# Rows of x, logits and routing matmuls of two groups of batches in the score banks of PSUM

## The chip, the core and the metric

The kernel runs on one core of one Trainium2 chip (trn2). The engines are PE (TensorE, the matmul engine), DVE (VectorE), ACT (ScalarE), POOL (GpSimd) and SP (SyncE, which here only issues DMAs). The metric is the device time of one execution in microseconds, the lower the better; three runs of the kernel before are shown, and one more execution was profiled.

## What is computed

Sparse attention of 8 batches, 8 heads, 576 positions and 64 dimensions a head is followed by a mixture of experts in which every token goes to one expert. Heads 0 to 3 see a local window of 32 positions, heads 4 to 7 every 32nd position. Cut to what matters:

```
scores = scale * q @ k.T                       # per batch and head
scores = where(mask, scores, -1e9)             # local (heads 0-3) or strided (heads 4-7)
attn   = softmax(scores) @ v
x      = attn.transpose(0, 2, 1, 3).reshape(4608, 512)
logits = x @ w_gate                            # 8 experts
expert, gate = argmax(logits), softmax(logits)[argmax]
for e in range(8):
    xe = x[expert == e]
    out[expert == e] = gate * (relu(xe @ w1[e]) @ w2[e])   # 512 -> 1024 -> 512
```

All is fp32. The expert products are made from two parts of each operand, a rounded one (hi) and the rest (lo), with three matmuls for each product: hi x hi, lo x hi, hi x lo.

## The kernel before

**Attention as tasks.** A task is one score bank: 512 columns that hold several blocks of queries and keys of one batch. Each batch has five (`BANK_PAIRS`), so there are 40 tasks in all; tasks 3 and 4 of a batch are scored together (`PAIR`). In one turn of the loop PE scores a task (mask matmul L439, then L450, L458 or L464), transposes the probabilities of the task three turns ago (L501, `LAG_T`) and multiplies those of the task four turns ago with V (L526 for local heads, L515 for strided ones, `LAG_AV`). Between a task's scores and its transposes stands the softmax: DVE takes the maximum (nm, L377) and subtracts it (prob, L380, the last reader of the score bank), ACT takes the exponential (L381), DVE sums (sm, L383; ri, L385 and L386), POOL multiplies (L387). ACT copies the products with V to xT (L166), which holds x of two batches, transposed.

**What follows a group.** Two batches make a group, so there are four. When a batch of a group is through, its *logits* (PE L576 with the gate's weights wg, DVE's copy ls at L162, PE's transposes L583, DVE's sum L584), its *rows of x* (`xrows`: PE transposes xT at L568, ACT copies the bank to xr at L166, a DMA issued by ACT at L571 writes the rows to xd in DRAM) and, after the second batch, the *route* (rank of each token in its expert: PE L618 and L620, DVE rk L623; lists of token numbers: PE L666, DVE idacc L669) are worked in small steps between the tasks of the following batches.

**Early experts.** From the third group on, PE's time between attention steps is filled with windows of experts 0, 2, 4 and 6 over the tokens of the first two groups. A window gathers rows of xd (xg, on POOL), transposes them (PE L296, in a v bank), splits them (ACT xh L240, DVE xl L241), and for each of four chunks of weights loads raw (1 MB, issued by SP at L221), splits it (ACT whi L231, DVE wlo L232, two halves each), makes the hidden product (PE L320 to L322 in a t bank), splits that (ACT hh L325, DVE hl L326) and makes the second product (PE L309 to L311 in y banks). At the end y is scaled (DVE L276 or ACT L274) and scattered by POOL.

**Tables and the rest.** When all groups are routed, `slot_tables` works out which tokens the remaining windows and slots take (DVE almost alone: the function from L727 on, with comparisons L803 and L808 at its end and PE's L812 in v banks for each group), between steps of the last early window and the first window of expert 0. Then come windows and slots of all experts to the end.

**PSUM.** All eight banks are given out by four tags with two banks each (`BANKS`, L58): s for scores, t for transposes and hidden products, v for products with V, and y for second products. A tag's two banks take turns, so an allocation waits until the content of the allocation two before it has been read. `XTAGS` (L59) gives, for each of the four groups, the tag that `xrows`, `logits` and `route` allocate.

**Order.** In the attention loop PE's order is the order of the program text (`tc.manual_schedule`). The orders of DVE, ACT, POOL and SP, and PE's after the loop, are made by the scheduler of the build, which estimates when each instruction could start. On the chip each engine runs its row in that order and waits where something isn't ready.

Of the kernel before, what the change touches and what calls it, by code (L numbers as in the profile page):

```python
# [55 lines left out]
X_ENG = "aa"  # L56
LS_ENG = "v"
BANKS = {"s": 2, "t": 2, "v": 2, "y": 2}  # L58
XTAGS = "yyvv"  # L59
YTAGS = "yyss"  # L60
PRE = (0, 2)
BANK_PAIRS = (
# [85 lines left out]
def moe_attn(ctx, tc, qk, vv, wg, wcat, blob0, blob, out):  # L148
# [8 lines left out]
    def bank(tag):  # L157
        return ps.tile([128, 512], F32, name=tag, bufs=BANKS[tag])
# [186 lines left out]
    with ExitStack() as actx:  # L345
# [217 lines left out]
        def xrows(g, c, xT):  # L563
            xr = xrp.tile([128, XW], F32, name="xr")
            nc.gpsimd.tensor_copy(out=xr[:, DM:XW], in_=gates[g][:, c:c + 1].broadcast_to([128, XW - DM]))
            xb = bank(XTAGS[g])
            for pr in range(4):
# [5 lines left out]
        def logits(g, c3, xT, L):  # L573
            lb = bank(XTAGS[g])
            for pr in range(4):
                nc.tensor.matmul(lb[32 * pr:32 * pr + 32, 0:384], wg_sb[:, pr, :], xT[:, pr, c3 * 384:(c3 + 1) * 384],  # L576
                                 start=True, stop=True, tile_position=(0, 32 * pr))
            ls = rt.tile([128, 384], F32, name="ls", bufs=2)
            evac(LS_ENG, ls, lb[:, 0:384])
            yield  # L580
            lt = bank(XTAGS[g])
            for i in range(3):
                nc.tensor.transpose(lt[:, i * 128:(i + 1) * 128], ls[:, i * 128:(i + 1) * 128], ident)  # L583
            nc.vector.tensor_reduce(out=L[:, 3 * c3:3 * c3 + 3, :],  # L584
                                    in_=lt[:, 0:384].rearrange("p (t q e) -> p t e q", t=3, q=4)[:, :, 0:E, :],
                                    axis=AX.X, op=ALU.add)
            cs = slice(3 * c3, 3 * c3 + 3)
            mx = rt.tile([128, 3], F32, name="mx", bufs=2)
            nc.vector.tensor_reduce(out=mx, in_=L[:, cs, :], axis=AX.X, op=ALU.max)
            dl = dls[g][:, cs, :]  # L590
            nc.vector.tensor_tensor(out=dl, in0=L[:, cs, :], in1=mx.unsqueeze(2).broadcast_to([128, 3, E]), op=ALU.subtract)
            ex = rt.tile([128, 3, E], F32, name="ex", bufs=2)
            nc.scalar.activation(out=ex, in_=dl, func=AF.Exp)
            yield
            gt = gates[g][:, cs]
            nc.vector.tensor_reduce(out=gt, in_=ex, axis=AX.X, op=ALU.add)
            nc.vector.tensor_scalar(out=gt, in0=gt, scalar1=1e-9, scalar2=None, op0=ALU.add)
            nc.vector.reciprocal(out=gt, in_=gt)
# [4 lines left out]
        def route(g):  # L603
# [9 lines left out]
            if g < NG - 1:  # L613
                yield
                yield
            rb = bank(XTAGS[g])
            rv = rb[:, 0:(GT + 1) * E].rearrange("p (c e) -> p c e", e=E)
# [43 lines left out]
            if g < NG - 1:  # L661
                yield
                yield
            ib = bank(XTAGS[g])
            for c in range(GT):
# [634 lines left out]
```

## Time and profile before

| | us |
|---|---|
| three runs: median (lowest to highest) | 630.91 (630.07 to 633.26) |
| the profiled execution | 629.62 |
| its span from first to last instruction | 627.7 |
| PE busy in the span | 589.2 (94%) |
| DVE busy | 374.2 (60%) |
| ACT busy | 296.3 (47%) |
| POOL busy | 159.3 (25%) |

The profile gives for each engine the time in which it ran instructions; waiting for a semaphore, issuing a DMA and branches aren't counted. Times in the trace are counted from the start of the span. An execution lasts 1.9 us longer than its span. PE is the busiest engine over the whole span, but the shares differ by stage: the last two groups of batches are worked from about 107 to 226 us, the tables from 226 to 268, the remaining windows from there to the end.

### The profile page before, as it was taken

What the parts mean: (1) busy time and instruction counts of PE and PEld (TensorE: products, weight loads), DVE (VectorE), ACT (ScalarE), POOL (GpSimd) and SP (SyncE); (2) the same over time, 40 slices, a digit from 0 to 9 for tenths busy, and PEclk for the clock granted to TensorE, in tenths of its full rate; (3) what the DMA queues carried; (4) which work ended last, traced back from release to release, by engine and by line L of the source; (5) the groups of instructions that cost most, each with busy time, mean ns of one, the idle gap of its engine ahead of it and who ended that gap; (6) DMA issues with size and microseconds to landing.
All of it is one profiled execution on the core that took longest, in us unless ns stands there. A gap on an engine that the chain in (4) does not pass through costs nothing. (4 is left out here: it accounts for less than half of the span.)

```text
span 627.7 us, 14487 instructions
## 1 busy us (share of the span) xinstructions
PE 589.2 (94%) x5973; PEld 491.2 (78%) x5986; DVE 374.2 (60%) x744; ACT 296.3 (47%) x523; POOL 159.3 (25%) x195
## 2 busy tenths in 40 slices
PE   4898897899889999899999999999999999999996
PEld 3676765678778888797888898788998878887885
DVE  6779989877573699987325855233634334551332
ACT  1676767754665544555325744233533324442241
POOL 3333432530230303146302432022412004020021
PEclk9999999999899999989999999999999999999999
DMA  8888999986458657469934774375655538253201
GB/s 316 269 307 294 300 359 317 374 299 237 158 176 314 209 191 244 153 229 331 393 144 149 250 263 172 117 252 187 212 191 184 173 105 296 107 175 144 69 32 58
DMA packets 33540, 137.25 MB, mean 219 GB/s; under 512 B 4666, under 2 KB 5056, under 8 KB 24768
## 3 DMA queue, kind: packets, MB, share of 16 engines
q1 hardware_dynamic: 19840, 93.33, 43.3%
q10 hardware_dynamic: 7344, 22.71, 9.9%
q0 software_dynamic: 6288, 20.26, 8.8%
q8 instruction: 48, 0.79, 0.5%
q14 instruction: 20, 0.16, 0.1%
HBM read 117.11 MB, written 19.63 MB: 218 GB/s over the span
## 5 line engine op out<-in xcount | busy, mean ns | idle before, releaser
L232 DVE TENSOR_TENSOR wlo<-raw,whi 128x1024 fp32r<-128x1024 f32 x112 | 135.0, 1225 | 69.7 <-ACT whi L231 67.5
L231 ACT CAST whi<-raw 128x1024 fp32r<-128x1024 f32 x112 | 114.2, 1050 | 58.2 <-PE s L311 39.8
L320 PE MATMUL t<-xh,whi 128*128 128x256 f32 (+2 forms) x384 | 131.8, 344 | 2.9 <-DVE hl L326 1.6
L322 PE MATMUL t<-xh,wlo 128*128 128x256 f32 (+2 forms) x384 | 128.1, 334 | 0.6 <-DVE wlo L232 0.6
L321 PE MATMUL t<-xl,whi 128*128 128x256 f32 (+2 forms) x384 | 128.1, 334 | 0.0
L326 DVE SCALAR_TENSOR_TENSOR hl<-t,hh 128x256 fp32r<-128x256 f32 (+2 forms) x96 | 52.0, 542 | 116.3 <-ACT hh L325 116.2
L325 ACT ACTIVATE hh<-t 128x256 fp32r<-128x256 f32 (+2 forms) x96 | 46.4, 483 | 138.8 <-PE t L322 137.7
L320 PEld LDWEIGHTS t<-xh,whi 128*128 128x128 f32 x384 | 72.6, 189 | 13.1 <-issue 3.2
L322 PEld LDWEIGHTS t<-xh,wlo 128*128 128x128 f32 x384 | 72.8, 190 | 6.2 <-DVE wlo L232 0.9
L321 PEld LDWEIGHTS t<-xl,whi 128*128 128x128 f32 x384 | 72.8, 190 | 6.2 <-DVE xl L241 0.3
L310 PE MATMUL y<-wlo,hh 128*128 128x512 f32 x192 | 76.0, 396 | 0.9 <-DVE wlo L232 0.9
L309 PE MATMUL y<-whi,hh 128*128 128x512 f32 x192 | 76.8, 401 | 0.0
L311 PE MATMUL y<-whi,hl 128*128 128x512 f32 x192 | 75.6, 396 | 0.0
L387 POOL TENSOR_TENSOR prob<-prob,ri 128x512 f32<-128x512 f32 x40 | 43.2, 1088 | 101.2 <-DVE ri L386 62.0
L277 POOL DMA_INDIRECT out_dram<-y,oids x27 | 29.7, 1099 | 106.0 <-DVE y L276 100.5
L249 POOL DMA_INDIRECT xg<-xd,ids x27 | 33.4, 1238 | 75.2 <-PE v L296 38.5
L311 PEld LDWEIGHTS y<-whi,hl 128*128 128x128 f32 x192 | 36.2, 189 | 8.3 <-DVE hl L326 0.8
L310 PEld LDWEIGHTS y<-wlo,hh 128*128 128x128 f32 x192 | 36.5, 190 | 6.5 <-DVE wlo L232 1.4
L309 PEld LDWEIGHTS y<-whi,hh 128*128 128x128 f32 x192 | 36.6, 191 | 5.8
L166 ACT COPY xT<-v 128x270 f32<-128x270 f32 (+1 forms) x80 | 29.2, 484 | 18.0 <-PE v L515 9.4
L381 ACT ACTIVATE prob<-prob 128x512 f32<-128x512 f32 x40 | 25.0, 632 | 20.4 <-DVE prob L380 20.1
L310 PE MATMUL s<-wlo,hh 128*128 128x512 f32 x88 | 34.6, 393 | 0.0
(226 smaller groups left out, 904.2 us busy)
## 6 DMA issues: line engine op xcount, KB each, us to landing
raw<-in_wcat_dram SPq DMA_DIRECT2D x56, 1024.0 KB, 5.3
sraw<-in_wcat_dram ACTq DMA_DIRECT2D x12, 1024.0 KB, 4.9
xd<-xr ACTq DMA_DIRECT2D x36, 264.0 KB, 4.0
qkl<-in_qk_dram SPq DMA_DIRECT2D x32, 264.0 KB, 4.8
vl<-in_vv_dram SPq DMA_DIRECT2D x16, 512.0 KB, 6.2
vt<-in_vv_dram SPq DMA_DIRECT2D x16, 256.0 KB, 5.8
qk<-in_qk_dram SPq DMA_DIRECT2D x8, 484.0 KB, 6.4
qk<-in_qk_dram SPq DMA_DIRECT2D x8, 432.0 KB, 5.6
```

The costliest lines, as they stand in the source:

```text
L231: nc.scalar.copy(out=hi[:, sl], in_=raw[:, sl])
L232: i = nc.vector.tensor_tensor(out=lo[:, sl], in0=raw[:, sl], in1=hi[:, sl].bitcast(F32), op=ALU.subtract)
L249: lastp[0] = nc.gpsimd.indirect_dma_start(out=xg, out_offset=None, in_=xd[0:rows, :], in_offset=bass.IndirectOffsetOnAxis(ap=idc, axis=0))
L309: nc.tensor.matmul(yb[t], hh[:, ts], whi[:, w], start=(j == 0), stop=False)
L310: nc.tensor.matmul(yb[t], hh[:, ts], wlo[:, w], start=False, stop=False)
L311: nc.tensor.matmul(yb[t], hl[:, ts], whi[:, w], start=False, stop=(j == 7))
L320: nc.tensor.matmul(hb[:, 0:n], whi[:, w], xh[:, dc, :], start=(dc == 0), stop=False)
L321: nc.tensor.matmul(hb[:, 0:n], whi[:, w], xl[:, dc, :], start=False, stop=False)
L322: nc.tensor.matmul(hb[:, 0:n], wlo[:, w], xh[:, dc, :], start=False, stop=(dc == 3))
L325: nc.scalar.activation(out=hh[:, 0:n], in_=hb[:, 0:n], func=AF.Relu)
L326: nc.vector.scalar_tensor_tensor(out=hl[:, 0:n], in0=hb[:, 0:n], scalar=0.0, in1=hh[:, 0:n].bitcast(F32), op0=ALU.max, op1=ALU.subtract)
L387: product[0] = nc.gpsimd.tensor_tensor(out=pv, in0=pv, in1=ri.unsqueeze(2).broadcast_to([128, 8, 64]), op=ALU.mult)
```

## The change

```
-XTAGS = "yyvv"
+XTAGS = "yyss"
```

For the first two groups nothing changes: their rows of x, logits and routes stay in y banks, which no early window needs yet. For the third and fourth group these three allocate s banks rather than v banks. They then take turns with the scores, not with products with V, with the windows' transposes L296 and with the tables' L812. `YTAGS`, which looks alike, gives the banks of windows' second products and isn't touched. The same instructions run on the same engines with the same sizes; only their banks differ, and the order that the scheduler makes on DVE, ACT, POOL and SP, and on PE after the loop.

On PE, in the turn of the third group at 115 to 119 us, the order is kept and the banks change (operation, then destination and sources, the letter ahead of the arrow being the bank's tag):

```order
 L526 MATMUL v<-pTl_137,vl 64x2x32 x16
 L526 MATMUL v<-pTl_138,vl 64x2x32 x16
-L568 MATMUL v<-cst_70,xT 128x128 x4
-L501 MATMUL t<-cst_70,prob 128x128 x4
-L568 MATMUL v<-cst_70,xT 128x128 x4
+L568 MATMUL s<-cst_70,xT 128x128 x4
+L501 MATMUL t<-cst_70,prob 128x128 x4
+L568 MATMUL s<-cst_70,xT 128x128 x4
 L439 LDWEIGHTS identb
 L439 MATMUL s<-mask_b,identb 128x512
 L450 MATMUL s<-qkl_136 32x2x64 x16
```

The two L568 now stand in one row with the scores L439 and L450 for the same two banks.

On DVE, at 172 to 178 us (numbers tell one buffer from the next; 3265 and 3276 belong to the two scores of a pair, 3346 to a hidden product, 3401 to half of a weight split), the row before reads:

```order
L232 TENSOR_TENSOR wlo_3401<-raw_3399,whi_3400 128x1024
L377 TENSOR_REDUCE nm_3265<-s_3229 128x8
L377 TENSOR_REDUCE nm_3276<-s_3230 128x8
L380 TENSOR_TENSOR prob_3267<-s_3229,nm_3265 128x512
L380 TENSOR_TENSOR prob_3278<-s_3230,nm_3276 128x512
L326 SCALAR_TENSOR_TENSOR hl_3346<-t_3332,hh_3345 128x256
L383 TENSOR_REDUCE sm_3270<-prob_3267 128x8
L669 TENSOR_TENSOR idacc_84<-v_3356,idacc_84 128x80
```

and with the change:

```order
L377 TENSOR_REDUCE nm_3265<-s_3229 128x8
L377 TENSOR_REDUCE nm_3276<-s_3230 128x8
L380 TENSOR_TENSOR prob_3267<-s_3229,nm_3265 128x512
L380 TENSOR_TENSOR prob_3278<-s_3230,nm_3276 128x512
L232 TENSOR_TENSOR wlo_3401<-raw_3399,whi_3400 128x1024
L383 TENSOR_REDUCE sm_3270<-prob_3267 128x8
L383 TENSOR_REDUCE sm_3281<-prob_3278 128x8
L385 TENSOR_SCALAR ri_3272<-sm_3270 128x8
L326 SCALAR_TENSOR_TENSOR hl_3346<-t_3332,hh_3345 128x256
```

The split moved behind the softmax's subtractions, and hl moved behind the split and both sums.

On ACT, in the table stage at 245 to 256 us (whi is a cast of a weight chunk, two halves; hh the activation of a hidden product), the row before reads:

```order
L231 CAST whi_4338<-raw_4337 128x1024 x2
L325 ACTIVATE hh_4319<-t_4306 128x256
L325 ACTIVATE hh_4358<-t_4345 128x256
L231 CAST whi_4408<-raw_4407 128x1024 x2
L325 ACTIVATE hh_4392<-t_4379 128x256
```

and with the change:

```order
L231 CAST whi_4338<-raw_4337 128x1024 x2
L325 ACTIVATE hh_4319<-t_4306 128x256
L231 CAST whi_4408<-raw_4407 128x1024 x2
L325 ACTIVATE hh_4358<-t_4345 128x256
L325 ACTIVATE hh_4392<-t_4379 128x256
```

The casts of the next chunk and the activation hh_4358 changed places.

On DVE at the same place, before:

```order
L232 TENSOR_TENSOR wlo_4339<-raw_4337,whi_4338 128x1024
L789 TENSOR_TENSOR t1_4368<-t1_4368,own_4304 128x36
L790 TENSOR_TENSOR skey_4300<-skey_4300,t1_4368 128x36
L792 TENSOR_TENSOR whole_4331<-t1_4368,whole_4331 128x36
L326 SCALAR_TENSOR_TENSOR hl_4359<-t_4345,hh_4358 128x256
```

and with the change:

```order
L789 TENSOR_TENSOR t1_4368<-t1_4368,own_4304 128x36
L232 TENSOR_TENSOR wlo_4409<-raw_4407,whi_4408 128x1024
L790 TENSOR_TENSOR skey_4300<-skey_4300,t1_4368 128x36
L326 SCALAR_TENSOR_TENSOR hl_4359<-t_4345,hh_4358 128x256
L791 SCALAR_TENSOR_TENSOR skey_4300<-t1_4368,skey_4300 128x36
```

The first half of the next chunk's split, wlo_4409, moved ahead of L790 and hl_4359.

## Rows read from the trace of the kernel before

**Rows 1.** Busy time by stretch: us, busy PE, PEld, DVE, ACT, POOL (instructions), PEclk, DMA share, GB/s.
```profile
107.00:226.00 119.00, 107.96 (x1462) 90.06 (x1466) 81.48 (x198) 69.96 (x138) 32.37 (x43) 0.99 0.70 248
226.00:268.00 42.00, 39.91 (x278) 35.76 (x277) 41.09 (x99) 21.20 (x33) 8.17 (x6) 0.99 0.57 196
268.00:627.70 359.70, 353.04 (x2088) 297.94 (x2087) 164.66 (x214) 139.16 (x216) 81.59 (x89) 0.99 0.52 185
```

**Rows 2.** Timeline: start, us, engine, line, operation, count, [idle before, releaser]; 107 to 111.
```profile
107.91 1.40 PE L576 MATMUL v<-xT,wg_sb 128*32 128x384 f32 x8 [0.70 <-ACT xT L166]
108.71 1.23 DVE L380 TENSOR_TENSOR prob<-s,nm 128x512 f32<-128x512 f32 x2
110.06 0.66 PE L501 MATMUL t<-cst,prob 128*128 128x128 f32 x4 [0.75 <-POOL prob L387]
```

**Rows 3.** Timeline, 116 to 123, PE, ACT and DVE.
```profile
116.05 0.59 ACT L166 COPY xr<-v 128x512 f32<-128x512 f32 x1
...
116.21 0.66 PE L568 MATMUL v<-cst,xT 128*128 128x128 f32 x4 [0.57 <-ACT xT L166]
...
118.74 1.07 ACT L166 COPY xr<-v 128x512 f32<-128x512 f32 x2 [0.67 <-PE v L568]
...
118.95 0.38 PE L439 MATMUL s<-mask_b,identb 128*128 128x512 bf16 x1
...
120.00 0.69 DVE L380 TENSOR_TENSOR prob<-s,nm 128x512 f32<-128x512 f32 x1
...
122.46 0.66 PE L296 MATMUL v<-cst,xg 128*128 128x128 f32 x4 [1.24 <-ACT xT L166]
```

**Rows 4.** Timeline, 128 to 133, DVE and PE.
```profile
128.58 1.21 DVE L232 TENSOR_TENSOR wlo<-raw,whi 128x1024 fp32r<-128x1024 f32 x1
...
132.05 0.55 PE L583 MATMUL v<-cst,ls 128*128 128x128 f32 x3 [1.07 <-DVE ls L162]
```

**Rows 5.** Timeline, 165 to 171, PE.
```profile
165.13 1.11 PE L568 MATMUL v<-cst,xT 128*128 128x128 f32 x4 [0.69 <-ACT xT L166]
...
170.88 0.38 PE L439 MATMUL s<-mask_b,identb 128*128 128x512 bf16 x1
```

**Rows 6.** Timeline, 172 to 178, PE and DVE.
```profile
172.03 0.21 PE L464 MATMUL s<-qk 64*54 64x54 f32 x1
...
174.10 1.28 DVE L377 TENSOR_REDUCE nm<-s 128x8 f32<-128x512 f32 x2
175.30 1.28 DVE L380 TENSOR_TENSOR prob<-s,nm 128x512 f32<-128x512 f32 x2
176.50 0.41 DVE L326 SCALAR_TENSOR_TENSOR hl<-t,hh 128x256 fp32r<-128x256 f32 x1
176.83 0.67 DVE L383 TENSOR_REDUCE sm<-prob 128x8 f32<-128x512 f32 x1
...
176.96 0.39 PE L320 MATMUL t<-xh,whi 128*128 128x256 f32 x1 [1.62 <-DVE hl L326]
```

**Rows 7.** Timeline, 186 to 188, PE.
```profile
186.84 0.66 PE L568 MATMUL v<-cst,xT 128*128 128x128 f32 x4 [0.28 <-ACT xT L166]
```

**Rows 8.** Timeline, table stage, 243 to 265: SP's queue, DVE, ACT and PE.
```profile
243.71 0.33 SPq L221 DMA_DIRECT2D raw<-in_wcat_dram  x1
...
250.11 0.18 DVE L789 TENSOR_TENSOR t<-t,own 128x36 f32<-128x36 f32 x1
...
250.62 0.39 ACT L325 ACTIVATE hh<-t 128x256 fp32r<-128x256 f32 x1 [2.63 <-PE t L322]
...
251.54 2.00 ACT L231 CAST whi<-raw 128x1024 fp32r<-128x1024 f32 x2 [0.53 <-DMA raw<-in_wcat_dram]
...
252.54 0.39 PE L309 MATMUL y<-whi,hh 128*128 128x512 f32 x1
...
264.92 0.53 PE L812 MATMUL v<-prob,am 128*128 128x86 bf16 x9 [1.45 <-DVE prob L808]
```

**Rows 9.** Busy time by stretch, columns as in rows 1: the stretch with clock 0.50.
```profile
164.70:168.10 3.40, 2.97 (x9) 2.56 (x10) 1.07 (x4) 2.00 (x6) 0.59 (x1) 0.50 0.72 290
```

## Prediction, made before the changed kernel had run

> **What bounds the kernel now.** I read the busy time by stage first [rows 1]: for three stretches it gives how long PE, the matmul engine, was busy. From 107 to 226 us, where the last two groups of batches are worked, PE is busy 107.96 of 119.00 us; from 226 to 268, where the slot tables are built, 39.91 of 42.00; from there to the end 353.04 of 359.70. So PE sets the end everywhere, and a stall of PE moves the end unless a later stall swallows it. From 107 to 268 PE idles 11.0 + 2.1 = 13.1 us; that is all that a change of banks could ever win, and most of that isn't about banks. The same rows show the exception: from 226 to 268 DVE is busy 41.09 of 42.00, so there DVE's row of work, not PE's, is what must not be delayed, and at the end PE waits 1.45 for it, at L812 [rows 8].
>
> Then I went through the rows of PE with idle time before them and asked which wait on a bank. An allocation of a tag gets the older of its two banks, so it waits until the content of two allocations ago has been read. In the v banks ACT copies of products with V do the reading, in the s banks DVE's subtraction in the softmax (L380) or, once rows of x go there too, ACT's copies of those rows. Three stalls of PE at L568 wait for ACT's copy of xT, which is a v bank: 0.57 [rows 3], 0.69 [rows 5] and 0.28 us [rows 7]. The change takes away 1.54 us of waits at most and puts waits on s in their place. It also moves work on DVE and ACT, since the scheduler orders these engines anew; PE's order stays as it is up to the table stage.
>
> **Part by part, attention.** All sums stand against the profiled execution, 629.62 us; the median of the three runs is 630.91, 1.29 more, and I add the same difference to both.
>
> First logits, at 107.91. L576 takes its bank from the first score of the pair, which the first of two L380 (108.71, two in 1.23) frees at 108.71 + 0.64 = 109.35, so it starts 1.4 later. Today its matmuls are through at 107.91 + 1.40 = 109.31 and L501 behind them waits until 110.06, 0.75 of it for POOL [rows 2], so 0.75 of the 1.4 is swallowed at once and up to 0.7 is left. Ends 0 and 0.7; I take **0**, since the stalls at 122.46 and 132.05 wait for other engines and would take up a delay that PE alone has.
>
> Rows of x between scores, 116 to 122. The 0.57 before L568 goes, but the score behind it needs a bank whose row is copied until 116.05 + 0.59 = 116.64, so nothing is won. The next L568 needs the bank of the first of two copies at 118.74, and the score at 118.95 needs the bank of the score before it, which L380 holds from 120.00 to 120.69 [rows 3]. That score starts at about 120.73, 1.78 later. The wait at 122.46, where L296 stands idle 1.24 for copies of xT, doesn't swallow this, because those copies follow the products, which follow the score; only what ACT was behind with its copies can be made good. I carry 1.4 of the 1.78 to the next stall. There, at 132.05, PE waits 1.07 for DVE's ls. ls stands behind a split of weights (wlo, 128.58, 1.21) that the scheduler now runs earlier, while DVE waits for the late score [rows 4], so DVE gets there less late than PE does, and part of the 1.07 absorbs the delay. Ends: 0.3 if all of it is absorbed, 1.4 if none. I take **+0.85**, the middle.
>
> At 165.13 the wait of 0.69 goes. What now comes next is the score at 170.88, which needs the copy of the row before it [rows 5]; this leaves it hardly any slack. Between -0.69 and 0, I take **-0.6**.
>
> At 176.96 PE stands idle 1.62 for hl. Before, DVE runs a split, two maxima (nm), two subtractions (prob) and then hl; now it runs the maxima first, then the subtractions, the split, two sums (sm) and ri, and only then hl. That frees the score banks earlier, as the route matmuls L666 need them, so these don't wait; but hl has two sums and ri ahead of it, 2 x 0.6 + 0.1 = 1.3 [rows 6]. The maxima can start when the scores end, at 172.03 + 0.21 = 172.24, rather than behind the split; the split itself stays ahead of hl. So between 1.3 - 0.65 and 1.3; I take **+1.0**.
>
> At 186.84 the wait of 0.28 goes [rows 7], and a short matmul of the last ranking stands before its neighbour instead of behind it: **-0.4** together, 0 at worst. Attention adds up to 0.85 - 0.6 + 1.0 - 0.4 = **+0.85**, ends -0.1 and, without what is said for the first step, 2.7.
>
> **The table stage.** PE moves eight transposes (L296) from inside the tables up to their start, where PE stands idle; it wins nothing, because at 264.92 PE waits 1.45 for DVE's L808 and would wait longer [rows 8]. What counts is ACT. Before, hh at 250.62 stands ahead of the two casts whi; now it stands behind them. The casts need a weight load issued at 243.71, and run from 251.54 to 253.54, released by the load's landing [rows 8]. So hh ends at about 253.9 instead of 251.0. PE's next product, at 252.54, needs that hh and the hl behind it: PE stalls some 1.9 us. DVE suffers the same: its split of these weights now stands right behind L789 (250.11, so reached at about 250.3) and needs the first cast, at 251.54 + 1.0 = 252.55: 2.2 idle, against 0.4 before. DVE has 0.9 us of idle in its 42, so nothing later takes it up; hl and L808 come that much later, and L812 with them. One y that DVE scales is pulled ahead of the last L808 and can add about 0.65. Ends 1.6 and 2.6, I take **+2.0**; it is 0 if the load lands some 2 us sooner, since then the casts are done when hh's product is.
>
> On the row, the load takes 251.5 - 243.7 = 7.8 us for 1 MB. The Trainium skill (DMA: Bandwidth & Descriptors, Where 436 GB/s comes from) holds about 358 GB/s for what binds loads from HBM on one core; an estimate by that is 1.05 MB / 358 = 2.9 us, which would land the load before 248 and make the sum +0.85. The measured row disagrees, since other loads share the queue, and the measurement decides.
>
> On POOL two gathers stand behind two more copies, and on SP one weight load stands ahead of two loads of attention; their buffers are long free and their readers late, so I cost both at 0. If this cover were gone, the price would be one such load. After 268 the order is unchanged.
>
> Sum: +0.85 + 2.0 = **+2.85**, that is 632.5 on the profiled execution and 633.8 on the median.
>
> **Rivals.** (a) *The load lands in time*, or DVE and ACT keep clear of each other: the table stage costs nothing, and +0.85 remains, 631.8. For it: PE and DVE come about 0.9 us late to this place while the load doesn't have to, and 2 us are enough. Against: the load's buffer is freed by the same engines, so it may shift with them. The Trainium skill's rate cited above (the same page and section) would give just this.
>
> (b) *A further stretch at half clock*, on the slow side. In 164.70 to 168.10 the granted clock is 0.50, the lower of two levels (1.2 GHz), and PE was busy 2.97 us in it [rows 9]; at the upper level that work would take half as long, so such a stretch costs up to 1.5 us. The one here comes after PE has idled. The change makes two new idle places, near 119 (1.8 us) and near 252 (1.9 us). If one of them brings a stretch of this kind, the forecast becomes 633.8 + 1.5 = 635.3. It decides when one of the new stalls is followed by 0.50 in the clock row. The Trainium skill (TensorE: Matmul & The Clock Gate, A second HAM failure mode: psum-queue depth-cycling) describes a kernel in which going round the PSUM banks left PE small idles and its clock oscillated between the two levels; the row at 164.70 agrees that it happens in this kernel.
>
> (c) *Faster.* The stretch at half clock at 164.70 doesn't come, since the wait of 0.69 beside it goes (-1.5), the waits at 165.13 and 186.84 are won (-1.0) and nothing is lost in the table stage or at 119: about -2.5 to -3.3, 627.6 to 628.4. For it: the idle goes exactly there. Against: PE idles elsewhere before that stretch too, where the change does nothing, and every one of these terms has to go well at once.
>
> (d) *Nothing moves*: banks were never what is waited for, new orders hide. 630.9. Against it speak three rows that wait on a v bank.
>
> **How the numbers follow.** Forecast: the ends add up to -0.1 + 1.6 = +1.5 and 2.7 + 2.6 = +5.3, and since not all upper ends come at once I cut this to +1.5 to +4.5: 0.48. (a) 0.22, (b) 0.15, (c) 0.08, (d) 0.07. A measurement of this kernel can tell about 0.5%, 3.15 us, from no change: 627.8 to 634.1. The forecast lies just under the upper bound, so of its 0.48 I put 0.22 above it; with 0.14 of (b) and 0.01 of (a) slower has 0.37. Faster is 0.05, most of (c). Same has the rest, 0.58. The range leaves out (c) and the outer ends: its low end is (a) with attention at its lower end, 630.9 - 0.1, less the 0.8 by which the runs shown scatter below their median, and some more for a won stretch in part: 629.3. Its high end is the forecast's +4.5 with a half-clock stretch, 630.9 + 4.5 + 1.5 = 636.9, taken as 637.0.
>
> **What would show it.** Right: L296 near 123 some 1.2 us later than now against the stretch's start; hl before 178 behind two sums; a stall of PE of about 2 us after 252 that ends with hh, right behind two casts that the load released; the last L812 about 3 us later. Wrong: the casts start without waiting for the load (rival a); clock rows of 0.50 where now they are 1.00, or 1.00 at 165 (b, c); scores near 119 that don't wait for L380.

## The result, and the profile after

The changed kernel took 637.94 us (median of 5, 632.76 to 640.18) and the kernel before, beside it, 631.17: the ratio is 1.0109, 95% interval 1.0077 to 1.014, some 6.9 us slower. A second comparison gave 1.0088, 1.0057 to 1.0119 (5.5 us); one execution in it, 640.21 us, counts as slow and is left out of that ratio and of the means below. The forecast was slower by 2.9 us, 633.8, with a range up to 637.0. So the sign was right, the forecast was about half of what was measured, and the median lies above the range.

The profiled execution of the changed kernel took 632.76 us, the least of those five, 3.14 over the 629.62 of before. Read alone it would confirm the sum of 2.85. It must not be read alone: two more traces of the changed kernel and two more of before were taken (below, changed_again, changed_look, b_again, before_look). The table gives how long each stretch lasted, from the start of one matmul to the start of another (named by its time in the first trace of before), as the mean of three traces each (from several chips):

| stretch | before | changed | difference | forecast |
|---|---|---|---|---|
| start to 100.77 | 101.21 | 102.05 | +0.8 | 0 (same program) |
| 100.77 to 132.05 | 31.77 | 32.46 | +0.7 | +0.85 |
| 132.05 to 165.13 | 33.22 | 32.34 | -0.9 | -0.6 |
| 165.13 to 188.04 | 22.70 | 23.79 | +1.1 | +0.6 |
| 188.04 to 251.23 | 63.20 | 63.53 | +0.3 | 0 |
| 251.23 to 296.17 | 44.68 | 48.30 | +3.6 | +2.0 |
| 296.17 to the end | 331.57 | 331.52 | -0.1 | 0 |
| span | 628.35 | 633.99 | +5.6 | +2.85 |

The first row scatters from 99.8 to 104.5 us over the changed kernel's traces, where both kernels still run the same instructions in the same order, and is chance. Attention (100.77 to 188.04) costs +0.9, where +0.85 was forecast, but the agreement is partly luck: in this stretch the changed kernel's traces spend 6.8 us at half clock in the mean and those of before 4.6, and the steps without the clock add up to less (below). The table stage costs nearly twice what was forecast, and nothing of it comes back after 296. It too has more half clock in it, 4.6 us against 1.1.

Busy time by stretch of the changed kernel, which answers to [rows 1] (columns as there):

```profile
107.00:226.00 119.00, 109.93 (x1468) 91.38 (x1466) 79.15 (x196) 68.81 (x135) 31.92 (x43) 0.97 0.69 244
226.00:268.00 42.00, 39.74 (x261) 34.88 (x259) 37.18 (x95) 19.11 (x31) 6.47 (x5) 0.96 0.55 198
268.00:630.90 362.90, 354.26 (x2108) 298.92 (x2108) 169.50 (x220) 141.20 (x219) 85.67 (x91) 1.00 0.52 184
```

DVE, busy 41.09 of 42.00 before, now is at 37.18: it waits. The mean granted clock is 0.97 and 0.96 in the first two stretches, where before it was 0.99.

The timeline of attention after, PE with one row each of ACT and DVE, which answers to [rows 2, 3, 4, 5, 6, 7]:

```profile
108.50 1.51 PE L576 MATMUL s<-xT,wg_sb 128*32 128x384 f32 x8 [0.81 <-DVE prob L380]
...
119.28 0.66 PE L568 MATMUL s<-cst,xT 128*128 128x128 f32 x4 [1.29 <-ACT xr L166]
...
120.66 0.39 PE L439 MATMUL s<-mask_b,identb 128*128 128x512 bf16 x1 [0.29 <-DVE prob L380]
123.72 0.66 PE L296 MATMUL v<-cst,xg 128*128 128x128 f32 x4 [0.78 <-ACT xT L166]
...
132.61 0.55 PE L583 MATMUL s<-cst,ls 128*128 128x128 f32 x3 [0.36 <-DVE ls L162]
...
164.94 0.66 PE L568 MATMUL s<-cst,xT 128*128 128x128 f32 x4
...
174.75 1.16 ACT L166 COPY pTl<-t 64x512 f32<-64x512 f32 x2
...
175.57 0.42 DVE L326 SCALAR_TENSOR_TENSOR hl<-t,hh 128x256 fp32r<-128x256 f32 x1
...
175.97 0.39 PE L320 MATMUL t<-xh,whi 128*128 128x256 f32 x1 [2.10 <-ACT pTl L166]
...
187.04 0.65 PE L568 MATMUL s<-cst,xT 128*128 128x128 f32 x4
...
215.03 0.66 PE L568 MATMUL s<-cst,xT 128*128 128x128 f32 x4 [1.07 <-ACT xr L166]
```

The waits on v at L568 are gone, and L576, L568 and L439 now wait for the readers of s banks, DVE's L380 and ACT's xr. At 175.97 PE waits for ACT's second copy pTl, which ends at 174.75 + 1.16 = 175.91, and no longer for hl, which ends at 175.57 + 0.42 = 175.99, after PE has started. All eight traces with these rows of the third group in s agree: L320 starts 0.05 to 0.06 us behind the end of that copy. In before it was hl: 176.50 + 0.41 = 176.91 against 176.96 [rows 6]. The wait at 215.03 is one that no step of the forecast had.

ACT, PE and DVE in the table stage after, which answers to [rows 8]:

```profile
252.79 1.99 ACT L231 CAST whi<-raw 128x1024 fp32r<-128x1024 f32 x2 [4.33 <-DMA raw<-in_wcat_dram]
...
253.87 1.23 DVE L232 TENSOR_TENSOR wlo<-raw,whi 128x1024 fp32r<-128x1024 f32 x1 [2.53 <-ACT whi L231]
...
254.69 0.65 ACT L325 ACTIVATE hh<-t 128x256 fp32r<-128x256 f32 x2
...
255.12 0.79 PE L309 MATMUL y<-whi,hh 128*128 128x512 f32 x1 [1.94 <-ACT hh L325]
...
260.19 0.42 DVE L326 SCALAR_TENSOR_TENSOR hl<-t,hh 128x256 fp32r<-128x256 f32 x1 [1.94 <-ACT hh L325]
...
269.76 0.53 PE L812 MATMUL v<-prob,am 128*128 128x86 bf16 x9 [1.97 <-DVE prob L808]
```

ACT idles 4.33 us for the load with a ready hh behind the casts in its queue; PE idles 1.94 for that hh. DVE idles 2.53 for the first cast and once more, 1.94, for the hh of a later hidden product. And the granted clock around it, which answers to [rows 9]:

```profile
251.72:255.13 3.41, 1.47 (x14) 1.26 (x12) 1.26 (x3) 2.34 (x4) 0.00 (x0) 1.00 0.75 220
255.13:258.54 3.41, 3.41 (x10) 2.83 (x11) 3.05 (x10) 0.21 (x1) 0.00 (x0) 0.50 0.54 171
258.54:261.95 3.41, 3.31 (x27) 2.88 (x27) 1.76 (x4) 1.20 (x2) 0.00 (x0) 1.00 0.63 262
```

Where PE restarts, the clock is at 0.50, the lower level: PE was busy 1.47 of the 3.41 us ahead. The first L309 takes 0.79 us there, where it took 0.39 in before [rows 8].

### The profile page after: what moved, and what is told of

The parts are those of the page before. It is cut to its first block, busy times and chain, and to the rows that moved or that the text cites. A ratio compares the mean times of both kernels' runs of the same rounds, so it can differ in the third digit from the quotient of the medians.

```text
span 630.9 us, 14490 instructions
## 1 busy us (share of the span) xinstructions
PE 592.3 (94%) x5986; PEld 492.2 (78%) x5986; DVE 374.1 (59%) x744; ACT 296.1 (47%) x523; POOL 161.3 (26%) x195
## 5 line engine op out<-in xcount | busy, mean ns | idle before, releaser
L320 PE MATMUL t<-xh,whi 128*128 128x256 f32 (+2 forms) x384 | 131.7, 344 | 2.9 <-ACT pTl L166 2.1
L322 PE MATMUL t<-xh,wlo 128*128 128x256 f32 (+2 forms) x384 | 128.1, 334 | 0.6 <-DVE wlo L232 0.6
L320 PEld LDWEIGHTS t<-xh,whi 128*128 128x128 f32 x384 | 72.8, 190 | 13.1 <-issue 3.2
L309 PE MATMUL y<-whi,hh 128*128 128x512 f32 x192 | 77.1, 402 | 1.9 <-ACT hh L325 1.9
L322 PEld LDWEIGHTS t<-xh,wlo 128*128 128x128 f32 x384 | 72.7, 190 | 6.8 <-DVE wlo L232 1.6
L277 POOL DMA_INDIRECT out_dram<-y,oids x27 | 29.5, 1091 | 105.3 <-DVE y L276 99.8
L249 POOL DMA_INDIRECT xg<-xd,ids x27 | 35.3, 1308 | 73.3 <-PE v L296 38.4
L309 PEld LDWEIGHTS y<-whi,hh 128*128 128x128 f32 x192 | 36.6, 191 | 7.9 <-ACT hh L325 2.1
L311 PE MATMUL s<-whi,hl 128*128 128x512 f32 x88 | 34.4, 391 | 0.0
```

The lines of the kernel that those rows point to most:

```text
L249: lastp[0] = nc.gpsimd.indirect_dma_start(out=xg, out_offset=None, in_=xd[0:rows, :], in_offset=bass.IndirectOffsetOnAxis(ap=idc, axis=0))
L309: nc.tensor.matmul(yb[t], hh[:, ts], whi[:, w], start=(j == 0), stop=False)
L311: nc.tensor.matmul(yb[t], hl[:, ts], whi[:, w], start=False, stop=(j == 7))
L320: nc.tensor.matmul(hb[:, 0:n], whi[:, w], xh[:, dc, :], start=(dc == 0), stop=False)
L322: nc.tensor.matmul(hb[:, 0:n], wlo[:, w], xh[:, dc, :], start=False, stop=(dc == 3))
```

## The experiments

Two theories were to be told apart. By **theory C** what the forecast lacks is clock: the new stalls bring more time at half clock, that is with TensorE's granted clock at 0.50. By **theory L** it is a weight load that lands late in some executions, and the clock only follows. Each execution comes with its span and mean granted clock; the time at half clock is 2 x (1 - clock) x span. It counts half clock wherever it stands, also in the first 25 us and at the very end, where all kernels run the same. All on one chip, save the first five runs of the changed kernel:

| kernel | executions | median us | ratio to before (95%) | us at half clock, mean |
|---|---|---|---|---|
| before | 58 | 630.1 to 630.8 | 1 | 13.5 |
| b_again (before itself) | 12 | 630.20 | 0.9993 (0.9971 to 1.0016) | 13.1 |
| changed kernel, both sets | 14 | 637.50 | 1.0109 and 1.0088 | 20.4 |
| third_only | 12 | 632.37 | 1.0023 (0.999 to 1.0055) | 16.3 |
| fourth_only | 9 | 635.64 | 1.0079 (1.005 to 1.0108) | 17.6 |
| hh_first | 11 | 635.22 | 1.0071 (1.0039 to 1.0102) | 20.9 |
| fourth_hh | 10 | 634.07 | 1.0053 (1.0028 to 1.0079) | 16.7 |
| logits_s | 12 | 630.78 | 1.0016 (0.9992 to 1.0039) | 13.5 |
| logits_v | 8 | 637.15 | 1.0093 (1.006 to 1.0125) | 17.9 |

The means at half clock are uncertain by 0.7 to 1.7 us (standard error). Within the kernels, an execution with 1 us more at half clock took 0.34 us longer (standard error 0.03, a line through the executions of all of them). This line doesn't say which makes which. In the first stretch, to 100.77, the four traces with 6.8 us at half clock at 14 to 24 us took 103.1 to 104.5 us, the six with 3.4 us there 100.8 to 101.9 and the four with none 99.5 to 101.9.

**b_again**, the kernel before, without an edit.

> The kernel before, unchanged, to see the mean granted clock of its executions. The changed kernel's five executions had mean clocks of 0.989, 0.984, 0.979, 0.984 and 0.982 with 632.8, 637.9, 640.1, 637.1 and 640.2 us. Theory C (the clock makes what the forecast lacks): the executions of before lie at 0.988 to 0.990, and within them the longer ones have the lower clock. Theory L (a late weight load in the table stage makes it, and the clock only follows): the clocks of before scatter as far down as 0.98, while its times stay within 630 to 633.

Measured: clocks from 0.985 to 0.996, times from 628.4 to 632.3, with the longer ones at 0.985 (632.34, 631.89 and 631.43). The clocks spread wider than theory C had said (0.988 to 0.990) and less far down than theory L had (0.98). Before's mean time at half clock, 13.1 us, is what its other runs show, and 7 us less than the changed kernel's 20.4. If the clock makes the time, at 0.34 us for each, that is 2.4 us of the 5.5 to 6.9: theory C can hold for a part, and more than half of the loss is something else.

**third_only** and **fourth_only** split the change by groups.

```
-XTAGS = "yyss"
+XTAGS = "yysv"     # third_only
+XTAGS = "yyvs"     # fourth_only
```

> Only the third group's rows, logits and route go through s; the table stage keeps the order of before. The steps of the forecast for this group, as the changed kernel's trace shows them, are +0.9 (scores near 119, left over after 132), -0.75 (165.13) and +0.6 (176.96): +0.7 in all, 631.9 us where the clock stays as before. If the new stall of 1.7 us near 119 sets off stretches at half clock (theory C with this stall as cause), the median lies at 634 to 636 and the mean clock at 0.984 or below. By theory L nothing beyond +0.7, since the load and its casts stay as they were.

> Only the fourth group goes through s; the attention of the third group stays as before and the table stage gets the order of the changed kernel (casts ahead of hh). By the forecast's steps -0.4 at 186.84 and +2.1 at the stall near 252.5: +1.7, 632.8 us where the clock stays as before. Theory C with the stall near 252 as cause: median 635 to 638 and mean clock at 0.984 or below. Theory L: the time scatters over 632 to 638 with the load's landing, and the stall near 252 differs between executions.

Measured: third_only +0.23% (1.5 us, not resolved), of which 2.8 us more at half clock x 0.34 = 1.0; what is left is 0.5, where +0.7 was expected. fourth_only +0.79% (5.0 us), of which the clock would explain 4.1 x 0.34 = 1.4. The loss sits with the fourth group and the order of the table stage; it is more than the 1.7 of the forecast's steps even without the clock. Its trace shows the stall, longer than in the first trace of the changed kernel (ACT and PE):

```profile
257.47 1.99 ACT L231 CAST whi<-raw 128x1024 fp32r<-128x1024 f32 x2 [5.15 <-DMA raw<-in_wcat_dram]
...
259.80 0.70 PE L309 MATMUL y<-whi,hh 128*128 128x512 f32 x1 [2.76 <-ACT hh L325]
```

and the clock ahead of and behind it:

```profile
256.52:259.93 3.41, 0.65 (x6) 0.44 (x5) 1.38 (x3) 2.46 (x4) 0.00 (x0) 1.00 0.69 286
259.93:263.34 3.41, 3.41 (x11) 2.83 (x12) 2.93 (x9) 0.09 (x1) 0.00 (x0) 0.50 0.23 38
```

**hh_first** puts one order of the changed kernel back: the first cast of the last early window's fourth chunk is placed behind the activation hh of its third chunk.

```
-            nc.scalar.copy(out=hi[:, sl], in_=raw[:, sl])
+            ci = nc.scalar.copy(out=hi[:, sl], in_=raw[:, sl]); [issue_after(ci, b) for b in behind]
...
-            whi, wlo = wsplit(*wload(e, c))
+            whi, wlo = wsplit(*wload(e, c), behind=hhs[4:5] if handover and e == EXP[-1] and c == 3 else ())
```

> The changed kernel with one order put back: on ACT the activation hh of the last early window (third chunk, first half) ahead of the casts of the fourth chunk, as before. The stall near 252.5 and DVE's idle there go, -2.1 to -2.6 against the changed kernel at equal clock. If that stall is what lowers the clock, the mean clock returns to 0.988 to 0.990 and the median to 631 to 632; if the stalls of attention do it, the clock stays at 0.984 or below and the median at 634 to 636. Theory L: back to 631.5 whatever the clock.

Measured: 635.22, against 637.50 of the changed kernel: -2.3 us at the same time at half clock (20.9 against 20.4), the size of the forecast's term for this place. By itself the difference isn't clear of noise (the means differ by 1.8, standard error 1.0); the trace carries the reading. The trace, ACT and PE at that place:

```profile
256.11 0.38 ACT L325 ACTIVATE hh<-t 128x256 fp32r<-128x256 f32 x1 [3.45 <-PE t L322]
258.19 1.99 ACT L231 CAST whi<-raw 128x1024 fp32r<-128x1024 f32 x2 [1.70 <-DMA raw<-in_wcat_dram]
...
259.29 0.39 PE L320 MATMUL t<-xh,whi 128*128 128x256 f32 x1 [0.54 <-ACT whi L231]
260.55 0.39 PE L322 MATMUL t<-xh,wlo 128*128 128x256 f32 x1 [0.76 <-DVE wlo L232]
...
272.00 0.53 PE L812 MATMUL v<-prob,am 128*128 128x86 bf16 x9 [1.94 <-DVE prob L808]
```

The load is late here too (the casts start at 258.19, 9.3 us after its issue at 248.90), but hh no longer stands behind them and PE waits only 0.54 + 0.76 for the chunk itself. What theory C expected of this place did not come true: the time at half clock stays at 20.9, so this stall isn't what makes the mean differ. In the trace the half clock behind 256 is gone (1.00), and comes at 273.74 instead, where a stretch of 0.50 stands in the first trace of before at 267.1 too.

```profile
255.90:259.30 3.40, 2.86 (x20) 2.27 (x18) 0.98 (x6) 1.49 (x3) 0.00 (x0) 1.00 0.87 284
259.30:262.70 3.40, 2.65 (x16) 2.31 (x17) 3.40 (x6) 1.55 (x3) 0.00 (x0) 1.00 0.10 41
273.74:277.15 3.41, 3.41 (x19) 3.41 (x18) 2.29 (x4) 0.38 (x1) 0.18 (x1) 0.50 0.72 190
```

**changed_again**, the changed kernel without an edit, and **fourth_hh**, which is fourth_only with the edit of hh_first.

> The changed kernel once more beside before, with more executions. Over 69 executions of six kernels the time follows the part of the span at half clock, 0.37 us for each us (about 1.25 us for a stretch of 3.4), and at no half clock before stands at 625.6, third_only at 626.3, fourth_only at 629.5, hh_first at 627.6. Theory C: the changed kernel has two stretches at half clock more than before in the mean (6.1 against 4.1) and stands at 629.5 to 630 without them, mean 636.5 to 638. If its first five executions were an accident: 633 to 634.

> fourth_only with hh put ahead of the casts, as in hh_first. fourth_only stood 3.9 us over before at equal clock, of which its profile shows 2.1 to 2.9 in the stall before L309. Forecast's steps: -0.4 (186.84), +0.2 (matmuls of the last group moved), +0.5 (last L812): +0.3 to +0.7 against before at equal clock, 4.1 to 4.5 stretches, 631 to 632. If the late weight load and not ACT's order makes the loss (theory L), it stays at 634 or more.

Measured: the changed kernel again 1.0088, so the first result was no accident; the mean clock is 0.984 again. fourth_hh 634.07, 1.6 us less than fourth_only (the means differ by 2.0, standard error 0.6), but 3.3 us (1.0053) over before where 0.3 to 0.7 was expected, and just at the 634 that theory L had named. Its trace shows the load late once more (L322 waits 0.76 for wlo, as in hh_first). 3.2 us more at half clock would make 1.1 of those 3.3 us; in its one trace the table stage takes 46.5 us, 1.8 over the mean of before's three. The rest isn't settled.

**logits_s** is the kernel before with the logits of the first batch of the third group in s. **logits_v** is the changed kernel with the logits of the third group back in v.

```
-            lb = bank(XTAGS[g])
+            lb = bank("s" if g == 2 and c3 == 0 else XTAGS[g])     # logits_s, on before
+            lb = bank("v" if g == 2 else XTAGS[g])                 # logits_v, on the changed kernel
```

(and the same for lt.)

> The kernel before with one edit: the first batch's logits of the third group (one L576 and one L583 after 107 us) take s banks, everything else stays. PE idles about 2.2 us before that L576 instead of 0.7, and the 0.75 before L501 goes: +0.7 us or nothing at equal clock. Theory C with this stall as one of its causes: a stretch at half clock follows the idle at 108 to 116 us, as in the profiles of the changed kernel, third_only and hh_first, the mean number of stretches rises from 4.1 to about 5, and the mean time by 1 to 2 us. If the stall doesn't matter for the clock: 0 to +0.7 and a mean clock of 0.989.

> The changed kernel with the logits of the third group back on v; rows and route stay on s. If the stall before L576 is what sets off the additional stretches at half clock: 5 stretches in the mean instead of 6.1, and 1 to 2 us less than the changed kernel. If the stall at 119 or the one near 252.5 sets them off, it stays with the changed kernel.

Measured: the stall came as expected, and so did the half clock behind it in the trace of logits_s (timeline, then busy time by stretch):

```profile
110.60 0.85 PE L576 MATMUL s<-xT,wg_sb 128*32 128x384 f32 x8 [2.29 <-DVE prob L380]
```

```profile
108.21:111.62 3.41, 1.12 (x13) 0.43 (x11) 3.04 (x9) 2.43 (x8) 1.04 (x1) 1.00 0.94 322
111.62:115.04 3.42, 3.42 (x40) 2.31 (x38) 3.31 (x12) 1.73 (x4) 1.19 (x2) 0.50 1.07 429
```

But over its twelve executions the time at half clock is 13.5 us, as before, and the median 630.78 (ratio 1.0016, not resolved). One trace misleads here: a third trace of before, which lacks this stall, has its half clock at 123.91 instead. And logits_v, which lacks it too, stays with the changed kernel in time (637.15); its 17.9 us at half clock are 2.5 less than the changed kernel's, which isn't clear of noise. So this stall costs a few tenths and is not the cause.

The trace of logits_v has the longest stall at L309 of all, with ACT's cast ahead of it:

```profile
258.01 1.99 ACT L231 CAST whi<-raw 128x1024 fp32r<-128x1024 f32 x2 [6.21 <-DMA raw<-in_wcat_dram]
...
260.34 0.79 PE L309 MATMUL y<-whi,hh 128*128 128x512 f32 x1 [3.82 <-ACT hh L325]
```

**changed_look** and **before_look**, one more trace of each kernel.

> The changed kernel for a third trace. In the four traces with the changed order of ACT the stretch from the matmul that before has at 251.23 to the L309 behind it lasted what the load's landing came after that matmul plus 2.43 us, to 0.01 (3.41, 3.79, 4.23 and 5.29 us at landings 0.98, 1.36, 1.80 and 2.86 late), and a stretch at half clock followed at once in each. Theory: the same here, 2.43 plus the lateness, and half clock right behind the stall. Otherwise that clock was chance: full clock for 3 us or more behind the stall.

> The kernel before once more, for its trace: when the weight load of the table stage lands against the matmul that the trace of before has at 251.23. In the two traces of before it landed 0.2 and 0.5 us after that; in the seven others 0.9 to 2.9 after. If the landing scatters in every kernel alike: anywhere from 0.2 to 2.5 here, and PE then waits at L320 and L322 only for what exceeds about 1 us. If the changed order makes the load late: 0.2 to 0.5 again.

The changed kernel's third trace, timeline and then busy time by stretch:

```profile
255.93 1.99 ACT L231 CAST whi<-raw 128x1024 fp32r<-128x1024 f32 x2 [4.88 <-DMA raw<-in_wcat_dram]
...
258.26 0.50 PE L309 MATMUL y<-whi,hh 128*128 128x512 f32 x1 [2.49 <-ACT hh L325]
```

```profile
255.51:258.92 3.41, 0.92 (x6) 0.54 (x5) 1.91 (x6) 2.54 (x4) 0.00 (x0) 1.00 0.66 267
258.92:262.33 3.41, 3.41 (x14) 3.03 (x13) 2.40 (x6) 0.00 (x0) 0.00 (x0) 0.50 0.35 98
```

In all five traces with the changed order of ACT (changed kernel three times, fourth_only, logits_v), L309 starts 2.33 us after the first cast: 255.12 - 252.79, 258.26 - 255.93, 259.80 - 257.47, 260.34 - 258.01, and 260.27 - 257.94 in changed_again. The casts start when the load has landed. So PE's stall there is the load's lateness plus a constant, and the load varies: from issue to cast 8.1 us in the first trace of the changed kernel, 8.5, 8.6, 8.9 and 10.0 in the others, 7.8 in the first trace of before, 9.9 in third_only. In before_look the load landed 1.0 us after the matmul that stands at 251.23 in the first trace, where it had been 0.2; PE didn't wait at L309, and 0.38 at L322. In third_only, with the order of before too, it landed 2.3 after, and PE waited 0.67 and 0.76.

But the lateness is not what the orders differ by. DVE, the limiting engine of this stage, needs the same casts for its split wlo and then goes on to the comparisons that PE's L812 waits for. From the first cast to the L812 with that wait it is 13.3 to 13.4 us in all seven traces with the order of before (264.92 - 251.54 = 13.38 in the first), 13.8 in the two with hh put back (272.00 - 258.19 = 13.81 in hh_first), and 16.9 to 17.0 in four of the five with the changed order (269.76 - 252.79 = 16.97 in the first; 17.8 in logits_v, where the half clock at the stall lasted twice as long). A late load costs each order its whole lateness; the changed order adds 3.6 us to that, and 0.4 of them stay with hh put back. So theory L doesn't explain the difference. One part of the lateness does belong to the change: the load is issued 7.0 us ahead of the matmul at 251.23 in the seven traces with the changed tables, with or without hh put back, and 7.4 to 7.5 in the seven others.

And at the stall the clock went to 0.50 in five of five traces, at its end or within 0.7 us of it; in the nine other traces, with the order of before or with hh put back, it was at 1.00 there. (Five of these nine have such a stretch later, at 267 to 274 us, and so have two of the five, at 276 and 277.) Behind it DVE waits a second time in all five, 1.9 us (2.8 in logits_v), for the hh of a product that PE makes late; none of the nine has this wait. No run has the stall without the half clock, so how the 3.2 us that hh_first takes back divide between the two is worked out and not shown.

**rows_late** and **rows_late_again** take from the change only what its trace showed to gain.

```
-            xb = bank(XTAGS[g])
+            xb = bank("s" if (g == 2 and c >= 3) or (g == 3 and c < 3) else XTAGS[g])
```

> The kernel before with only those rows of x in s banks that the trace of the changed kernel showed to gain: the second batch's rows of the third group (after 165) and the first batch's rows of the fourth (after 186.8). Logits, route and the rows near 116 stay on v, the table stage keeps its order, so none of the three new stalls (108, 119, 252.5) is there. Expected -0.75 at 165 and -0.4 at 186.8, with up to +0.6 at 176.96 where hl is placed as in the changed kernel: -0.5 to -1.1 against before, and the mean of four stretches at half clock as before. If the additional stretches come with s banks in any place and not with the stalls: 1 to 2 us slower and five or six stretches.

> rows_late once more beside before: -0.8 us in the first comparison (0.9989, interval 0.9969 to 1.001), and its trace is 0.7 us shorter between 132 and 165 (32.35 against 33.08, 33.46 and 33.11 in three traces of before). If that gain is real, 0.997 to 0.999 again, and the two comparisons together lie below 1. If it is chance: 1.000 to 1.002.

Measured: 629.05 us, ratio 0.9989 (0.9969 to 1.001), and in the second comparison, on another chip, 0.9973 (0.9951 to 0.9995), a gain of some 0.2%, resolved in the second alone. The time at half clock is 11.0 and 11.7 us against 12.0 and 14.8 of before beside it. The trace of rows_late shows where it comes from: L568 without the wait of [rows 5], while L320 waits 2.05 us, about as in the first trace of the changed kernel. The stretch from 132.05 to 165.13 lasts 32.3 to 32.4 us in all eight traces with these rows in s and 33.1 to 33.5 in the six others.

```profile
165.06 0.76 PE L568 MATMUL s<-cst,xT 128*128 128x128 f32 x4
...
177.51 0.39 PE L320 MATMUL t<-xh,whi 128*128 128x256 f32 x1 [2.05 <-ACT pTl L166]
```

So s banks don't cost clock by themselves, and this version has the lowest ratio of those tried.

## Why the prediction was right and wrong

**What bounds the kernel**: right. The part behind 296 took 331.3 to 331.6 us in all traces, so what PE had lost by then stayed lost.

**Logits at 107.91**: taken as 0, ends 0 and 0.7. L576 waits for L380 as forecast, 2.0 to 2.3 us at full clock (2.29 in logits_s) rather than 0.70, and the 0.75 before L501 is gone. The net in logits_s, 0.16%, is not resolved.

**Rows of x, 116 to 122**: right in place and size. Ahead of the step the delay against before is -0.31 (L568 at 115.90 against 116.21). The score at 120.66 is then 2.0 later than before (forecast 1.78), L296 at 123.72 is 1.6 later (forecast 1.4), and at L583 the delay is +0.56, so 0.87 stays, where 0.85 was taken as the middle.

**165.13**: right, from +0.56 to -0.19, -0.75 where -0.6 was taken. **186.84**: right, -0.37 where -0.4 was taken. **176.96**: wrong in the wait, and sized too high at +1.0. hl does stand behind two sums and ri, but PE isn't released by it any more; it waits for ACT's second copy pTl. PE's idle grew from 1.62 to 2.10, +0.5, below the lower end of 0.65.

These steps add up to 0.87 - 0.75 + 0.5 - 0.37 = about +0.25 in the first trace. The +0.9 of the table has some 2.3 us more at half clock in it, 0.8 us at 0.34 each, so the sum of +0.85 came out partly by luck.

**Missed in between**: rows of the last group wait 1.07 for ACT's xr at L568 (215.03); the eight transposes that PE now runs earlier fill its stall of 0.93 at 223, which the forecast held for worthless. Together +0.3.

**The table stage**: the mechanism was right and the term of +2.0 mis-sized; this is the step that failed. From the first cast to the L812 that PE waits for, the changed order takes 16.97 us and that of before 13.38, so it costs 3.6 us however late the load lands. With hh put back it is 13.81: 3.2 of the 3.6 come with the swap on ACT. The stall itself is what was said, 1.94 in the first trace where 1.9 was worked out, and DVE's idle 2.53 where 2.2 was. What the sum lacked, by the traces, is the clock behind it. Rival (b), a further stretch at half clock behind a new stall, stood beside the forecast with 0.15; in five of five traces it came with the stall at L309. In the first trace the delay against before grows through it from +2.58 (255.12 against 252.54) to +4.23 (259.22 against 254.99), 1.65 us, a little over the 1.5 that the rival had worked out from the row at 164.70, and DVE, which was taken to be busy from there on, waits 1.94 at 260.19. The likeliest case should have had both: 2.85 + 1.5 = 4.35. That leaves 1.2 to 2.6 of the 5.5 to 6.9 us; some 0.5 is the later issue of the load against PE, which no step had, and the rest isn't located.

The load's landing was read from one execution, 7.8 us after its issue, and that was among its earliest; the five traces of the changed order have 8.1 to 10.0, and PE's wait at L309 is 1.94 to 3.82, 2.7 in the mean. This makes PE's stall there longer than forecast, but by the times to L812 it costs the kernel before as much. By the 358 GB/s of the Trainium skill (DMA: Bandwidth & Descriptors, Where 436 GB/s comes from) the load would take 2.9 us (an estimate); no trace here agrees, with 7.8 to 10.0 us. The prediction put the slow landing down to other loads in the queue; in the trace of before SP issues none between this one and 250.27, and what moves beside it is POOL's gathers and scatters, 0.9 MB.

**Rival (b) over the whole execution**: also beyond that one place the changed kernel spends more time at half clock, 7 us in the mean with that place; this goes with some 2.4 us of time. Which stalls do it isn't settled. It is not the one at L576 alone (logits_s: none more) nor the one at L309 alone (hh_first: as many). The Trainium skill (TensorE: Matmul & The Clock Gate, A second HAM failure mode: psum-queue depth-cycling) tells of a kernel whose clock went up and down with small idles; the runs agree that it varies, and that its mean differs from kernel to kernel (13.1 and 13.5 us for before, 20.4 for the changed one), but not that cycling through banks is enough: rows_late cycles the s banks too, and has 11.0.

**Rivals (a), (c) and (d)** are out: the load never landed in time, the half clock at 164.70 didn't vanish but in two of three traces moved behind the longer stall at 175.97 (to 176.6 in the first), and both comparisons lie clear of no change.

**Numbers**: 0.37 stood on slower by over 0.5%. The upper end of the range, +4.5 and one stretch at half clock, was 6.0 over the kernel before; the first comparison gave 6.9 and the second 5.5, so the miss of the range is narrow.

## What to carry to other kernels

A change of banks changes two things: which reader frees a bank, and the order that a scheduler makes on all engines from then on. Here the steps of the banks came to a fraction of a microsecond in the first trace, each forecast to within half a microsecond, and a swap of one cast and one activation far behind them, in a stage that the edit doesn't touch, cost 3.2 us by the next place where PE waits. So compare the orders to the end of the program. Where an instruction that waits for a DMA has moved ahead of one that doesn't, price the stall, and add the half clock if the trace shows it behind stalls like it. How late the load lands takes several traces to know, and it counts in a difference only where the two orders pass it on differently.

One trace gives the places, not the mean: here the first trace of the changed kernel was the fastest of five executions. Before a stall in one trace is made the cause, look at the mean clock over all executions of a kernel that has this stall alone.

## What the runs showed of the hardware that was not expected

The wait from a load's issue to its first reader varied from 7.8 to 10.0 us for the same 1 MB at the same place of the program. The first 100 us, the same program in every kernel, took 99.5 to 104.5 us over the 14 traces. And the time at half clock in one execution is 13 to 14 us in the mean for the kernel before, yet its executions spread from 627.6 to 635.1 us, as much as this change is worth; 0.34 us of time go with each us of it, less than the 0.5 that half speed would cost if PE alone set the time. One stretch can be priced directly: from the L812 with the wait to the next L812 it is 7.8 us where the clock stays at 1.00 (266.91 to 274.72 in b_again) and 9.3 where a stretch at 0.50 falls between them (264.92 to 274.27 in before), 1.5 us more.
